# Remainders of the token blocks and of the second weight set on VectorE during the plain products, and a conversion's first two operations never in one step

## The chip, the cores and the metric

One core of one Trainium2 chip. The time is the device time of one execution in microseconds (us); the number quoted is the median of repeated runs. The engines are TensorE (PE in the profile; PEld is its weight load), VectorE (DVE), ScalarE (ACT), GpSimd (POOL) and SyncE (SP), which issues the transfers. Each engine works through its own queue in order; between engines only data dependencies hold work back.

## The reference

Relative-position attention, then a three-way maximum layer. Shapes: batch 4, 8 heads, 576 positions, head size 64; 2304 tokens, model width 512, inner width 768.

```python
scores = scale * q @ k.T + bias          # bias from |i - j| by a small MLP
attn = softmax(scores)                   # rows
x = (attn @ v) as [2304 tokens, 512]
h = max(max(x @ w1, x @ w2), x @ w3)     # 2304 x 768
out = h @ w_out                          # 2304 x 512
```

The three weight matrices and w_out arrive as 64-bit floats.

## The kernel before, in words

**Stages.** Bias setup (to about 57 us); attention, with the conversion of the 64-bit weights beside it (57 to 320 us); products of the tokens with w1, w2, w3 (321 to 525 us); products with w_out (525 us to the end).

**High and low parts.** A product in 32-bit precision is made of three products in a rounded type: a tile is split into a high part (a ScalarE copy that rounds) and a remainder (tile minus high part, a tensor_tensor by the helper `arith`, L415 to L417). Every such remainder, every sum and every elementwise maximum is recorded under L417, so the rows tell them apart by tile names: `b11l` is the remainder of block b11, `wl` that of a weight set, a bare `t` a sum.

**Attention steps.** `Attention.step(n, more)` (L367) is called for n = 0 to 84. Step n emits: the score matmuls of one tile of 128 rows for two heads (`front`, L254; every fifth tile holds the left-over rows of both heads); one to three pieces of attn @ v (`pv`, L347); per head VectorE's `sn` (L264) and ScalarE's exponential `e` (L276); then the side work handed in as `more`, one `next` per entry (L388); then VectorE's reciprocal `rc` (L286) with GpSimd's scaling of `e` (L289) for the step before; the copies of finished pv sums out of PSUM (`split_x`, L363, tile `xb`); and the transposes of step n - 5 (`flip`, L308, L317) with their copies `et` (ScalarE L403, L404; VectorE L406). The pv sum has one PSUM buffer, so the first pv piece of a new sum waits for the `xb` copy of the last. One sum ends in each step with n % 5 == 0, and its copy stands in VectorE's queue behind that step's side work; the next sum begins in the step after.

**Side work.** Generator `first` (`w0`) converts weights. `convert` (L462) is one ScalarE operation (L465: the absolute value, called A here) and four on VectorE (L467 "max", L469 "shift", L472 "or", L475 "fin"), with a yield after each. From step 10 on every step takes one `next` of it, and steps with n % 5 in (0, 4) take two. `early_x` prepares parts of token block 0 from step 45 on, each third step; `late_x` splits b21 and b22 of block 0 (ScalarE high, GpSimd remainder) from step 78 on.

**Token blocks.** The tokens' x is cut into three blocks (x = 0, 1, 2) of four tiles b11, b12, b21, b22 (128 x 768). The class `Blocks` (L423) makes their parts, and four sums t1 to t4 of them, each split as well.

**Weight products.** `moe` (L513) runs 54 items: weight set s times block x. For s = 0 `plain` (L528) multiplies directly, eight `slot()` calls per block. For the others `group` (L539) makes seven products p1, p5, p6, p7, p2, p4, p3 from blocks and sums, one slot after each; each product is 6 matmuls of 384 columns. ScalarE copies p1 and p5 out of PSUM, VectorE adds the others; eight PSUM banks rotate. A slot runs the jobs that stand in the table `jobs` under (item, slot), filled with `at(n, k, ...)` (L584). Slot jobs only set the order of each engine's queue; a later engine can run ahead of TensorE or behind it. Items 0 to 2 are the plain ones; item 3 is set 1 with block 0, and so on. Set 1's parts come from `raise_w` (two ScalarE copies, 768 and 1024 columns) and `lower_w` (remainders). `reload` fetches parked sets from DRAM into the buffers that set 1 leaves.

Of the kernel before, what the change touches and what calls it, by code (L numbers as in the profile page):

```python
# [19 lines left out]
def kernel(  # L20
# [12 lines left out]
    nc = tc.nc  # L33
# [137 lines left out]
    def load_bias(hp, t):  # L171
        if t < NTQ:
            nc.sync.dma_start(out=bias_t[t], in_=bias_rows(128 * t, 128, 2 * hp, 0, S, 2))
        else:
            nc.sync.dma_start(out=bias_t[t][0:LEFT], in_=bias_rows(LB, LEFT, 2 * hp, 0, S))
            nc.sync.dma_start(out=bias_t[t][64:64 + LEFT, 0:LB], in_=bias_rows(LB, LEFT, 2 * hp + 1, LEFT, LB))
            nc.sync.dma_start(out=bias_t[t][64:64 + LEFT, LB:S], in_=bias_rows(LB, LEFT, 2 * hp + 1, 0, LEFT))
# [5 lines left out]
    NS = NTQ + 1  # L183
# [5 lines left out]
    NSTEP = len(sched)  # L189
    LAG = NS  # L190

    class Attention:
# [174 lines left out]
        def step(self, n, more=()):  # L367
            m, f = n - 1, n - LAG
            nh = 0
            if n < NSTEP:  # L370
                un, t = fronts[n]
                hp, b = units[un]
                if t == 0 and un and un + 2 < len(units):
                    self.load_qk(un + 2)
                if t == 3 and un:
                    self.load_v(un)
                nh = self.heads(n)
                self.front(n)
            if n < NS:
                self.warm(n)  # L380
            for _ in range((1, 3, 2, 2, 2)[n % NS]):
                if self.pvq and n >= LAG + TS + 1:
                    self.pvq.pop(0)()
            back = 0 <= f < NSTEP
            for h in range(nh):
                self.shift(n, h)
                self.expo(n, h)
            for w in more:  # L388
                next(w, None)
            if n < NSTEP and b == border[-1] and hp + 1 < HP:  # L390
                load_bias(hp + 1, t)
            if 0 <= m < NSTEP:
                self.norm(m)
            if n < NSTEP and un + 1 < len(units):
                t0 = 1 if un == 1 else 0
                if t == t0:
                    self.splits = self.prep(un + 1)
                if t0 <= t < t0 + 2:
                    next(self.splits)
            self.split_x()  # L400
            if back:
                tps, left = self.flip(f)
                nc.scalar.copy(*tps[0])  # L403
                nc.scalar.copy(*left)  # L404
                if len(tps) > 1:
                    nc.vector.tensor_copy(*tps[1])  # L406
            if back:
                un, t = sched[f]
                g = 0 if t < TS else 1
                w = 128 * TS if g == 0 else S - 128 * TS  # L410
                if t in (TS - 1, NS - 1):
                    self.queue_pv(un, 128 * TS * g, w, *self.et)


    def arith(eng, out, a, b, op=ALU.subtract):  # L415
        f = lambda x: x.bitcast(F32) if x.dtype == F32R else x
        eng.tensor_tensor(out=out, in0=f(a), in1=f(b), op=op)  # L417
# [44 lines left out]
    def convert(pool, w, out, name):  # L462
        a = pool.tile([128, 512], F32, tag="wa", bufs=1, name=f"wa{name}")
        high, low, t = w[:, :, 1], w[:, :, 0], a.bitcast(U32)
        nc.scalar.activation(a, high.bitcast(F32), ACTF.Abs, scale=2.0 ** 16)  # L465
        yield
        nc.vector.tensor_scalar(out=a, in0=a, scalar1=2.0, scalar2=None, op0=ALU.max)  # L467
        yield
        nc.vector.tensor_scalar(out=t, in0=t, scalar1=3, scalar2=0x7FFFFFFF,  # L469
                                op0=ALU.logical_shift_left, op1=ALU.bitwise_and)  # L470
        yield
        nc.vector.scalar_tensor_tensor(out=t, in0=low, scalar=29, in1=t,  # L472
                                       op0=ALU.logical_shift_right, op1=ALU.bitwise_or)
        yield
        nc.vector.scalar_tensor_tensor(out=out, in0=high, scalar=signm, in1=t,  # L475
                                       op0=ALU.bitwise_and, op1=ALU.bitwise_or)
        yield
# [20 lines left out]
    def part(t, n):  # L498
        return t[:, 256 * n:256 * n + 256]
# [13 lines left out]
    def moe(pool, wpool, x0, xa, xb, raw, sr):  # L513
        ht = pool.tile([128, NX, 5, TW], F32, name="ht", bufs=1)
        hd = h_d.rearrange("(f p) (t n) -> p f t n", p=128, t=2)
        xb_ = [x0] + [Blocks(x, xa, xb) for x in range(1, NX)]
        v, g = nc.vector, nc.gpsimd
# [66 lines left out]
        def at(n, k, *what):  # L584
            jobs.setdefault((n, k), []).extend(what)

        b0, b1, b2 = xb_
        F = lambda f, *a: (lambda: f(*a))
        for k, what in enumerate((
                (F(b1.high, "b11", "b21"),),  # L590
                (F(b1.low, "b11"), F(b1.low, "b21", g)),
                (F(b1.high, "b12", "b22"),),
                (F(b1.low, "b12"), F(b1.low, "b22", g)),
                (F(b2.high, "b11", "b21"),),
                (F(b2.low, "b11"), F(b2.low, "b21", g)),
                (F(b2.high, "b12", "b22"),),
                (F(b2.low, "b12"), F(b2.low, "b22", g)),
                (F(b0.high, "t4"), F(b1.sum, "t1")),
                (F(b0.low, "t4"), F(b1.high, "t1")),
                (F(b1.low, "t1"), F(b1.sum, "t3")),  # L600
                (F(b1.high, "t3"), F(b1.sum, "t2")),
                (F(b1.low, "t3"),),
                (F(b1.sum, "t4"), F(b1.high, "t2"), F(b1.low, "t2", g)),
                (F(b2.sum, "t1"),),
                (F(b2.high, "t1"),),
                (F(b1.high, "t4"), F(b2.low, "t1")),
                (F(b1.low, "t4"),),
                (F(b2.sum, "t3"),),
                (F(b2.high, "t3"), F(b2.sum, "t2")),
                (F(b2.low, "t3"),),  # L610
                (F(b2.sum, "t4"), F(b2.high, "t2")),
                (F(b2.low, "t2"),),
                (),
        )):
            at(k // 8, k % 8, *what)
        at(3, 0, F(b2.high, "t4"))
        at(3, 2, F(b2.low, "t4"))

        made_w = {}

        def raise_w(s, k):
# [5 lines left out]
            else:  # L627
                nc.scalar.copy(wf[s][0][:, 768:1792], sr)

        def lower_w(s, k):  # L630
            raw, sr = made_w[s]
            hi, lo = wf[s]
            r = slice(256 * k, 256 * k + 256)
            arith(g, lo[:, r], part(raw, k + 1) if k < 3 else part(sr, k - 3), hi[:, r])

        def reload(s, k):
            if k == 0:
# [3 lines left out]
            nc.sync.dma_start(out=made_w[s][k], in_=w_d[s - PARK[1], k])  # L641

        made_w[1] = (raw, sr)
        at(1, 2, F(raise_w, 1, 0))
        at(1, 7, F(raise_w, 1, 1))
        for k, (n, y) in enumerate(((1, 3), (1, 4), (1, 6), (2, 1), (2, 2), (2, 4), (2, 6))):
            at(n, y, F(lower_w, 1, k))
        at(0, 0, F(reload, 2, 0))
        at(2, 0, F(reload, 3, 0))
        at(2, 7, F(reload, 2, 1))  # L650
# [1 line left out]
        for s in range(2, NSET):  # L652
            n = 3 * s - 3
# [34 lines left out]
        for s in range(4, NSET):  # L688
            n = 3 * s - 8
# [30 lines left out]
        n = 3 * NSET - 3  # L720
# [35 lines left out]
        n = 3 * NSET - 2  # L756
# [22 lines left out]
        for k in range(NK):  # L779
# [10 lines left out]
            for y in range(parts):  # L790
                r = slice(y * DM // parts, (y + 1) * DM // parts)
# [10 lines left out]
    with tc.manual_schedule():  # L802
# [3 lines left out]
        at = Attention(apool)  # L806
        n = 0
# [30 lines left out]
        last = {}  # L838

        def first():  # L840
# [5 lines left out]
            def conv(out, name):  # L846
                if todo:
                    ahead.append(fetch(wpool, *todo.pop(0)))
                yield from convert(wpool, ahead.pop(0), out.bitcast(U32), name)
# [35 lines left out]
        x0 = Blocks(0, xa, xa)  # L885

        def early_x():
            g = nc.gpsimd
            x0.high("b12")
            yield  # L890
            x0.low("b12", g)
            yield
            x0.high("b11")
            yield
            x0.low("b11", g)
            yield
            x0.sum("t1")
            yield
            x0.high("t1")
            yield  # L900
            x0.low("t1", g)
            yield

        def late_x():
            x0.high("b21")
            yield
            x0.low("b21", nc.gpsimd)
            x0.high("b22")
            yield
            x0.low("b22", nc.gpsimd)  # L910
            yield

        ex, lx = early_x(), late_x()
        while n < NSTEP + LAG:
            more = [w0] if n >= 2 * NS else []
            if n >= 2 * NS and n % NS in (0, 4) and n < NSTEP:
                more.append(w0)
            if n >= 9 * NS - 1 and n % 3 == 0:
                more.append(ex)
            if n >= NSTEP - 2:  # L920
                more.append(lx)
            at.step(n, more)
            n += 1
        while at.pvq:
# [6 lines left out]
        x0.sum("t2")  # L931
        x0.low("t3")
        at.split_x()
        x0.sum("t4")
        x0.high("t2")
        x0.low("t2", nc.gpsimd)
        apool.release()
        psums.pop().release()
        psums.append(ctx.enter_context(tc.tile_pool(name="psum_m", bufs=1, space=PSUM, reuse_waits="tile")))
# [57 lines left out]
```

## Time and profile before

| | us |
|---|---|
| median of 3 runs | 606.13 (605.68 to 606.67) |
| profiled execution | 606.03 |
| its span in the trace | 604.2 |

The profiled execution is 1.83 us longer than its span, which is what lies around the span, and 0.10 us under the median. Engine times overlap; only what TensorE waits for, or what it runs at a lower clock, can be read as lost directly.

### The profile page before, as it was taken

What the parts mean: (1) busy time and instruction counts of PE and PEld (TensorE: products, weight loads), DVE (VectorE), ACT (ScalarE), POOL (GpSimd) and SP (SyncE); (2) the same over time, 40 slices, a digit from 0 to 9 for tenths busy, and PEclk for the clock granted to TensorE, in tenths of its full rate; (3) what the DMA queues carried; (4) which work ended last, traced back from release to release, by engine and by line L of the source; (5) the groups of instructions that cost most, each with busy time, mean ns of one, the idle gap of its engine ahead of it and who ended that gap; (6) DMA issues with size and microseconds to landing.
All of it is one profiled execution on the core that took longest, in us unless ns stands there. A gap on an engine that the chain in (4) does not pass through costs nothing.

```text
span 604.2 us, 12112 instructions
## 1 busy us (share of the span) xinstructions
PE 583.6 (97%) x4360; PEld 469.6 (78%) x4360; DVE 438.3 (73%) x891; ACT 347.2 (57%) x800; POOL 330.1 (55%) x325
## 2 busy tenths in 40 slices
PE   8999999989999999999999989999999999999997
PEld 4456766666667666666668989999999999988886
DVE  7995778777788898887638779998999766722211
ACT  7997887878778888888756362223122122232322
POOL 2703765857555777768445546769677865600000
PEclk9999999999999999999999989999999999999999
DMA  5897455724584267510010042242113211754541
GB/s 169 245 333 266 151 159 163 239 85 163 160 249 139 71 192 205 152 38 21 22 36 1 1 140 69 89 140 69 36 57 119 88 36 35 227 184 142 169 149 70
DMA packets 70188, 76.70 MB, mean 127 GB/s; under 512 B 23152, under 2 KB 51184, under 8 KB 70128
## 3 DMA queue, kind: packets, MB, share of 16 engines
q1 hardware_dynamic: 69984, 75.64, 40.4%
q8 instruction: 34, 0.56, 0.4%
q10 hardware_dynamic: 144, 0.29, 0.2%
q14 instruction: 26, 0.21, 0.1%
HBM read 49.56 MB, written 26.36 MB: 126 GB/s over the span
## 4 chain that ended last, share of the span: by engine, by line
PE 67%; DVE 7%; issue 2%; ACT 2%; POOL 1%; DMA 1%; DVEq 0%; ACTq 0%; POOLq 0%
PE p L526 10%; PE pv L347 10%; PE p L524 10%; PE p L525 10%; PE tp L308 8%; PE s L254 7%; PE o L795 4%; PE o L798 4%; PE o L796 4%; DVE t L417 1%; DVE sn L264 1%; PE lp L317 1%; DVE b12l L417 1%; DVE xb L363 1%; DMA w64o<-in_moe_w_out_dram 1%
## 5 line engine op out<-in xcount | busy, mean ns | idle before, releaser
L289 POOL TENSOR_SCALAR e<-e,rc 128x576 f32<-128x576 f32 x144 | 106.1, 749 | 71.9 <-DVE rc L286 41.3
L276 ACT ACTIVATE e<-sn,nm 128x576 f32<-128x576 f32 x144 | 111.0, 773 | 43.5 <-DVE nm L264 41.0
L264 DVE CUSTOM_DVE_ANT_0 sn<-s,bias 128x576 f32<-128x576 f32 x128 | 91.7, 754 | 29.5 <-PE s L254 27.7
L308 PEld LDWEIGHTS tp<-ident,e 128*128 128x128 f32 x576 | 61.4, 141 | 36.0 <-issue 24.0
L308 PE MATMUL tp<-ident,e 128*128 128x128 f32 x576 | 81.2, 281 | 1.8 <-ACT et L403 0.8
L347 PE MATMUL pv<-et,vt 128*64 128x256 f32 (+1 forms) x496 | 73.6, 417 | 8.2 <-DVE xb L363 8.1
L553 ACT COPY m<-p 128x384 f32<-128x384 f32 x24 | 11.5, 481 | 90.2 <-PE p L526 40.9
L406 DVE COPY et<-tp 128x512 f32<-128x512 f32 x64 | 43.8, 685 | 22.5 <-PE tp L308 22.4
L254 PE MATMUL s<-kh,qh 64*128 64x288 f32 (+1 forms) x288 | 57.4, 343 | 1.5 <-ACT bs L158 0.9
L223 POOL TENSOR_TENSOR kl<-kr,kh 128x640 fp32r<-128x640 f32 x16 | 35.5, 2220 | 42.6 <-ACT kh L222 42.5
L347 PEld LDWEIGHTS pv<-et,vt 128*64 128x64 f32 x496 | 31.0, 136 | 30.4 <-issue 9.2
L417 DVE TENSOR_TENSOR hl<-hin,hh 128x768 fp32r<-128x768 f32 x18 | 18.2, 1010 | 50.1 <-ACT hh L751 50.1
L561 POOL TENSOR_TENSOR q<-mp,m 128x768 f32<-128x768 f32 x18 | 33.3, 1848 | 33.3 <-DVE mp L417 32.3
L403 ACT COPY et<-tp 128x512 f32<-128x512 f32 x80 | 45.9, 574 | 6.4 <-PE tp L308 6.4
L254 PE MATMUL s<-kl,qh 64*128 64x288 f32 (+1 forms) x288 | 48.8, 293 | 0.0
L254 PE MATMUL s<-kh,ql 64*128 64x288 f32 (+1 forms) x288 | 48.2, 290 | 0.0
L417 DVE TENSOR_TENSOR ht<-ht,q 128x768 f32<-128x768 f32 x36 | 45.5, 1303 | 0.0
L795 PE MATMUL o<-woh,hh 128*128 128x512 f32 (+1 forms) x114 | 43.4, 385 | 0.0
L138 PE MATMUL bp<-hid,w2s 128*32 128x79 f32 (+51 forms) x640 | 41.1, 391 | 2.1 <-DVE hid L117 1.8
L796 PE MATMUL o<-wol,hh 128*128 128x512 f32 (+1 forms) x114 | 43.0, 381 | 0.0
L254 PEld LDWEIGHTS s<-kh,qh 64*128 64x128 f32 (+1 forms) x288 | 31.5, 184 | 13.5 <-issue 7.1
L799 ACT COPY ot<-o 128x512 f32<-128x512 f32 (+1 forms) x19 | 10.7, 564 | 54.1 <-PE o L798 54.1
(175 smaller groups left out, 1534.9 us busy)
## 6 DMA issues: line engine op xcount, KB each, us to landing
bias_d<-bs SPq DMA_DIRECT2D x36, 295.5 KB, 5.9
bias<-bias_d SPq DMA_DIRECT2D x16, 576.0 KB, 4.1
w<-in_moe_w_dram SPq DMA_DIRECT2D x36, 256.0 KB, 3.9
h_d<-ht SPq DMA_DIRECT2D x18, 384.0 KB, 2.8
hin<-h_d SPq DMA_DIRECT2D x18, 384.0 KB, 3.9
qr<-in_qd_dram SPq DMA_DIRECT2D x16, 320.0 KB, 4.8
kr<-in_kd_dram SPq DMA_DIRECT2D x16, 320.0 KB, 5.0
out_dram<-ot SPq DMA_DIRECT2D x17, 256.0 KB, 4.0
```

The lines of the kernel that those rows point to most:

```text
L254: nc.tensor.matmul(ss[h][:, x, 0:HALF], lhsT=u[q][p, r], rhs=u[k][p, c:c + HALF], start=(j == 0), stop=(j == 2))
L264: nc.vector.tensor_tensor_reduce(out=sn.rearrange("p (a b) -> p a b", a=2), in0=st["s"][h][:, :, 0:HALF], in1=bt.rearrange("p (a b) -> p a ...
L276: nc.scalar.activation(st["e"][:, S * h:S * h + S], sn, ACTF.Exp, scale=-1.0, bias=nm, accum_out=st["sm"][:, h:h + 1])
L289: nc.gpsimd.tensor_scalar(out=e, in0=e, scalar1=rc[:, h:h + 1], scalar2=1.0, op0=ALU.mult, op1=ALU.mult)
L308: nc.tensor.transpose(tp[:, 128 * c:128 * c + 128], e2[:, k0:k0 + 128], ident)
L347: nc.tensor.matmul(pv[p], lhsT=w, rhs=x, start=(c == 0), stop=(c == NTQ))
L417: eng.tensor_tensor(out=out, in0=f(a), in1=f(b), op=op)
L524: nc.tensor.matmul(o, lhsT=hi[:, c], rhs=h[:, j], start=first and j == 0, stop=False)
L525: nc.tensor.matmul(o, lhsT=hi[:, c], rhs=l[:, j], start=False, stop=False)
L526: nc.tensor.matmul(o, lhsT=lo[:, c], rhs=h[:, j], start=False, stop=last and j == 1)
L795: nc.tensor.matmul(po, lhsT=hh[:, f], rhs=woh[:, r], start=(f == 0), stop=False)
L796: nc.tensor.matmul(po, lhsT=hh[:, f], rhs=wol[:, r], start=False, stop=False)
```

## The change

1. In `step`: if a side job that was just advanced yields "scalar", no further side job is advanced in that step. `convert` yields "scalar" after A. So A and the VectorE "max" that reads it never stand in one step, and later calls shift by one each time this bites.
2. `early_x` is put ahead of the conversion calls; `late_x` runs from step 82 on (before: 78), also first.
3. In the plain products every remainder of blocks 1 and 2 is on VectorE (five were on GpSimd: b21l and b22l of blocks 1 and 2, t2l of block 1), t2l of block 0 as well, and all seven remainders of weight set 1 move from GpSimd to two wide VectorE operations (768 and 1024 columns).
4. Order of the jobs: blocks 0's t4 sum and t2 parts move from ahead of `moe` into slots of item 0; set 1's copies to (2, 2) and (2, 3), its remainders to (2, 4) and (2, 5); the last sums of block 2 to items 3 and 4.

```diff
+            last = None
             for w in more:
-                next(w, None)
+                if last != "scalar":
+                    last = next(w, None)
...
         nc.scalar.activation(a, high.bitcast(F32), ACTF.Abs, scale=2.0 ** 16)
-        yield
+        yield "scalar"
...
-        def lower_w(s, k):
-            raw, sr = made_w[s]
+        def lower_w(s, k, eng=g, n=1):
+            src, o = (made_w[s][0], 256) if k < 3 else (made_w[s][1], -768)
             hi, lo = wf[s]
-            r = slice(256 * k, 256 * k + 256)
-            arith(g, lo[:, r], part(raw, k + 1) if k < 3 else part(sr, k - 3), hi[:, r])
+            r = slice(256 * k, 256 * (k + n))
+            arith(eng, lo[:, r], src[:, r.start + o:r.stop + o], hi[:, r])
...
+                (F(b1.high, "b11", "b21"), F(b0.sum, "t4")),
+                (F(b1.low, "b11"), F(b1.high, "b12"), F(b0.high, "t2")),
+                (F(b1.low, "b21"), F(b1.high, "b22")),
+                (F(b1.low, "b12"),),
+                (F(b1.low, "b22"), F(b2.high, "b11")),
+                (F(b0.low, "t2"), F(b2.high, "b21")),
+                (F(b1.sum, "t1"), F(b2.high, "b12")),
+                (F(b2.low, "b11"), F(b2.high, "b22"), F(b1.high, "t1")),
+                (F(b2.low, "b21"), F(b0.high, "t4")),
+                (F(b2.low, "b12"),),
+                (F(b2.low, "b22"),),
+                (F(b0.low, "t4"),),
+                (F(b1.low, "t1"),),
+                (F(b1.sum, "t3"),),
+                (F(b1.sum, "t2"), F(b1.high, "t3")),
+                (F(b1.low, "t3"),),
+                (F(b1.sum, "t4"), F(b1.high, "t2")),
+                (F(b1.low, "t2"), F(b1.high, "t4")),
+                (F(b1.low, "t4"), F(raise_w, 1, 0)),
+                (F(b2.sum, "t1"), F(raise_w, 1, 1)),
+                (F(lower_w, 1, 0, v, 3), F(b2.high, "t1")),
+                (F(lower_w, 1, 3, v, 4),),
+                (F(b2.low, "t1"),),
+                (F(b2.sum, "t3"),),
         )):
             at(k // 8, k % 8, *what)
-        at(3, 0, F(b2.high, "t4"))
-        at(3, 2, F(b2.low, "t4"))
+        at(3, 0, F(b2.sum, "t2"), F(b2.high, "t3"))
+        at(3, 1, F(b2.low, "t3"))
+        at(3, 3, F(b2.sum, "t4"), F(b2.high, "t2"))
+        at(3, 4, F(b2.low, "t2"))
+        at(3, 5, F(b2.high, "t4"))
+        at(4, 2, F(b2.low, "t4"))
...
-        at(1, 2, F(raise_w, 1, 0))
-        at(1, 7, F(raise_w, 1, 1))
-        for k, (n, y) in enumerate(((1, 3), (1, 4), (1, 6), (2, 1), (2, 2), (2, 4), (2, 6))):
-            at(n, y, F(lower_w, 1, k))
...
+            if n >= 9 * NS - 1 and n % 3 == 0:
+                more.insert(0, ex)
             if n >= 2 * NS and n % NS in (0, 4) and n < NSTEP:
                 more.append(w0)
-            if n >= 9 * NS - 1 and n % 3 == 0:
-                more.append(ex)
-            if n >= NSTEP - 2:
-                more.append(lx)
+            if n >= NSTEP + 2:
+                more.insert(0, lx)
...
         at.split_x()
-        x0.sum("t4")
-        x0.high("t2")
-        x0.low("t2", nc.gpsimd)
```

The old table of jobs of the plain products stands in the kernel above (L589 to L617).

## Rows read from the trace of the kernel before

**Rows 1.** The page's busy times: us, share of the span, instructions.

```profile
PE 583.6 (97%) x4360; PEld 469.6 (78%) x4360; DVE 438.3 (73%) x891; ACT 347.2 (57%) x800; POOL 330.1 (55%) x325
```

**Rows 2.** Who waited for whom: total us, times, longest us.

```profile
PE pv L347 <- DVE xb L363: 8.1, 7, 1.7
...
DVE wa L467 <- ACT wa L465: 3.7, 2, 1.9
```

**Rows 3.** TensorE's timeline, first pv pieces: start, us, instruction, [idle before <-releaser].

```profile
96.71 1.57 PE L347 MATMUL pv<-et,vt 128*64 128x320 f32 x10 [1.51 <-DVE xb L363]
...
129.81 1.84 PE L347 MATMUL pv<-et,vt 128*64 128x320 f32 x12 [1.66 <-DVE xb L363]
...
162.75 1.83 PE L347 MATMUL pv<-et,vt 128*64 128x320 f32 x12 [1.51 <-DVE xb L363]
...
179.37 1.83 PE L347 MATMUL pv<-et,vt 128*64 128x320 f32 x12 [0.82 <-DVE xb L363]
...
195.15 1.83 PE L347 MATMUL pv<-et,vt 128*64 128x320 f32 x12
...
211.48 1.84 PE L347 MATMUL pv<-et,vt 128*64 128x320 f32 x12
...
261.75 1.83 PE L347 MATMUL pv<-et,vt 128*64 128x320 f32 x12 [0.84 <-DVE xb L363]
...
277.43 1.83 PE L347 MATMUL pv<-et,vt 128*64 128x320 f32 x12
```

**Rows 4.** VectorE's timeline in four of the attention steps.

```profile
95.84 0.43 DVE L467 TENSOR_SCALAR wa<-wa 128x512 f32<-128x512 f32 x1 [1.86 <-ACT wa L465]
...
193.80 0.74 DVE L475 SCALAR_TENSOR_TENSOR wso<-w64o,signm,wao 128x512 uint32<-128x512 uint32 x1
...
210.15 0.42 DVE L467 TENSOR_SCALAR wao<-wao 128x512 f32<-128x512 f32 x1
210.60 0.43 DVE L469 TENSOR_SCALAR wao<-wao 128x512 uint32<-128x512 uint32 x1
...
222.57 1.88 DVE L467 TENSOR_SCALAR wa<-wa 128x512 f32<-128x512 f32 x1
```

**Rows 5.** TensorE's timeline, end of attention.

```profile
306.91 0.63 PE L308 MATMUL tp<-ident,e 128*128 128x128 f32 x4 [0.57 <-ACT et L404]
```

**Rows 6.** TensorE's timeline, items 3 to 5 (first product of each, and the waits).

```profile
346.46 0.34 PE L524 MATMUL p<-b11h,wh 128*128 128x384 f32 x1
...
349.14 0.44 PE L524 MATMUL p<-t1h,wh 128*128 128x384 f32 x1 [1.46 <-ACT wh L628]
...
357.64 0.44 PE L524 MATMUL p<-b11h,wh 128*128 128x384 f32 x1
...
365.05 0.34 PE L524 MATMUL p<-b11h,wh 128*128 128x384 f32 x1
...
372.35 0.34 PE L524 MATMUL p<-b11h,wh 128*128 128x384 f32 x1
```

**Rows 7.** Busy us (instructions) per engine by stretch, granted clock, DMA share, GB/s.

```profile
321.40:346.50 25.10, 25.10 (x145) 25.10 (x146) 20.13 (x13) 13.80 (x22) 16.70 (x9) 1.00 0.00 1
...
352.00:353.00 1.00, 1.00 (x5) 1.00 (x4) 0.96 (x2) 0.09 (x1) 1.00 (x2) 0.50 0.00 0
```

**Rows 8.** VectorE's timeline in the plain products and after.

```profile
321.25 0.95 DVE L417 TENSOR_TENSOR t<-xb,t 128x768 f32<-128x768 f32 x1
...
330.92 2.60 DVE L417 TENSOR_TENSOR b12l<-xb,b12h 128x768 fp32r<-128x768 f32 x1
...
335.97 0.95 DVE L417 TENSOR_TENSOR t4l<-t,t4h 128x768 fp32r<-128x768 f32 x1
```

**Rows 9.** GpSimd's timeline: beside a conversion, and in the plain products.

```profile
222.35 1.83 POOL L417 TENSOR_TENSOR b11l<-xb,b11h 128x768 fp32r<-128x768 f32 x1
...
330.14 2.56 POOL L417 TENSOR_TENSOR b21l<-xb,b21h 128x768 fp32r<-128x768 f32 x1
...
349.16 4.25 POOL L417 TENSOR_TENSOR wl<-ws,wh 128x256 fp32r<-128x256 f32 x4 [2.70 <-ACT wh L628]
```

More of the change, by code (lines that the diff above doesn't have):

```diff
@@ L585, in at @@
             jobs.setdefault((n, k), []).extend(what)
[L587 to L615, printed above, removed]
-        at(3, 0, F(b2.high, "t4"))
-        at(3, 2, F(b2.low, "t4"))
         made_w = {}
@@ L628, in raise_w @@
                 nc.scalar.copy(wf[s][0][:, 768:1792], sr)
-        def lower_w(s, k):
-            raw, sr = made_w[s]
+        def lower_w(s, k, eng=g, n=1):
+            src, o = (made_w[s][0], 256) if k < 3 else (made_w[s][1], -768)
             hi, lo = wf[s]
-            r = slice(256 * k, 256 * k + 256)
-            arith(g, lo[:, r], part(raw, k + 1) if k < 3 else part(sr, k - 3), hi[:, r])
+            r = slice(256 * k, 256 * (k + n))
+            arith(eng, lo[:, r], src[:, r.start + o:r.stop + o], hi[:, r])
+        b0, b1, b2 = xb_
+        F = lambda f, *a: (lambda: f(*a))
+        for k, what in enumerate((
+                (F(b1.high, "b11", "b21"), F(b0.sum, "t4")),
[22 more added lines that the diff above has]
+                (F(b2.sum, "t3"),),
+        )):
+            at(k // 8, k % 8, *what)
+        at(3, 0, F(b2.sum, "t2"), F(b2.high, "t3"))
[4 more added lines that the diff above has]
+        at(4, 2, F(b2.low, "t4"))
         def reload(s, k):
```

## The prediction

> **What bounds the kernel now.** First the page's busy times: TensorE is busy in 97% of the span [rows 1], so only its waits, or a lower clock, can be won; the other engines have room. Next the list of who waited for whom: in attention TensorE's largest wait is for VectorE's copy `xb`, 8.1 us in seven waits, and VectorE itself waited for A, ScalarE's first operation of a conversion; the row for `wa` has two such waits, and two more like it stand on `wao` [rows 2]. Then TensorE's timeline at the first pv pieces of a sum, to see which waits are long [rows 3]: three of 1.51 to 1.66 us (4.68 together), four of about 0.8 (the remaining 3.4), and none at 195.15, 211.48 and 277.43. Last, TensorE's timeline where the plain products end: item 3 starts at 346.46, stops 1.46 us before p5 and lasts until 357.64 (11.18 us), where item 5 takes 7.30 (365.05 to 372.35) [rows 6]. The windows show why a 1.5 us gap cost more: at 352 us the granted clock was 0.50, which is 1.2 of 2.4 GHz, after TensorE had stood still at 347.7 to 349.1 [rows 6, 7].
>
> So the change can win in two places: 8.1 us of pv waits, and 11.18 - 7.30 = 3.88 us in item 3.
>
> **The skip of a conversion call.** I counted the yields from step 10 on. In the steps with n % 5 == 0, whose VectorE work stands ahead of `xb`, the two calls give before: A and max in steps 15, 25, 35; two VectorE operations in 40 (shift, or), 50 (max, shift), 55, 60, 65 (or, fin); one in 45; none in 20, 30, 70. That is the pattern of the waits [rows 3]: the three long ones follow 15, 25 and 35, the four shorter ones 40, 55, 60, 65; after 45 (one, 195.15), 50 (211.48) and 70 (277.43) there is none. After the change: step 15 A alone; 25 and 35 fin, then A; 40, 55, 60, 65 max and shift; 50 A alone; 45 and 70 or and fin; 20 and 30 as before.
>
> - Steps 15, 25, 35: VectorE sat 1.86 us before max until A came [rows 4]. That goes. What is left is nothing or one fin, 0.74 us in its row, after which no wait followed (at 195.15) [rows 3, 4]: gain 4.68.
> - Steps 40, 55, 60, 65: or and fin become max and shift, 0.42 and 0.43 [rows 4], a pair after which no wait is shown at 211.48 [rows 3]. I leave 0.1 each for what the row can't resolve: 3.4 - 0.4 = gain 3.0.
> - Steps 45 and 70 get the pair or, fin that costs about 0.8 elsewhere [rows 3]: loss 1.6. Bounds: 0 (were there more slack) and 2.0.
> - Smaller: from 96.71 to 277.43 are eleven units, 180.72 us; at the wait-free unit of 15.68 (261.75 to 277.43) they would be 172.5 [rows 3]. The difference of 8.2 is 1.6 more than the six waits between (8.1 - 1.5), so ends of waits and late copies lose something that no row names. I take 0.4 as won, bounds 0 and 1.6.
>
> Moved past: where A goes a step later it lands in a step with no more ScalarE casts than steps 15, 25 and 35 had (A and one high part of k). The conversion has 75 steps and 28 double calls for 88 yields; even with each of its 14 A ending a step it is through by step 74, before the attention ends. The fetches and stores that stand in it go out up to five steps later on SP; nothing in attention reads them.
>
> **late_x four steps later.** TensorE waited 0.57 us at 306.91 for ScalarE's `et`, ahead of which `late_x` had put the high part of b22 [rows 5]. That goes to steps without exponentials. Gain 0.57. The cover: steps 82 to 84 are the last three, some 3.1 us each (15.68 / 5); GpSimd's two remainders there take about 1.83 us each [rows 9] with nothing else queued. Were they late, item 0 would wait for b21 by as much.
>
> **Plain products.** GpSimd's remainders and VectorE's hold each other up: a VectorE operation on 128 x 768 took 2.60 us at 330.92 beside GpSimd's 2.56, and 0.95 where GpSimd was idle (335.97) [rows 8, 9]. After the change GpSimd has no job from its last b22l to the first group's `q`. VectorE has, from the t4 sum (321.25 before [rows 8]) up to the second wide weight remainder, 22 operations; at 0.95, and 0.3 more for the 1024-wide one, 21.2 us; I add 2 us for four places where it waits for a ScalarE high part that stands behind a PSUM copy. So set 1's last remainder is ready at 321.25 + 23.2 = 344.5 on the old axis. TensorE needs it in p5, one product (7.30 / 7 = 1.04) and two matmuls after 346.46: 347.8. Slack 3.3 us, so the wait of 1.46 and the half-clock matmuls behind it go: item 3 falls to 7.30, gain 3.88. Before, the last of these remainders was on GpSimd until 349.16 + 4.25 = 353.4 [rows 9].
>
> Costed at nothing: ScalarE's highs, same number, 13.80 of 25.1 us busy before [rows 7]; block 2's t2, t3, t4 sums and remainders in items 3 and 4 (five or six times 0.95 to 1.5 beside adds of half a us), needed in item 5, whose t2 product is over two items after item 3 starts, 16 us; the eight PSUM banks cover a VectorE that is some us late. If that cover went, the price would be one late product per us. SP: the reloads into set 1's buffers wait for its remainders, which end 8.9 us earlier (353.4 to 344.5), so set 2 comes sooner; nothing new is queued behind them.
>
> **Sum.** 4.68 + 3.0 - 1.6 + 0.4 + 0.57 + 3.88 = 10.9 us. From the profiled execution, 606.03: 595.1; it is 0.10 under the median, so 595.2. After item 3 TensorE runs without a wait until the output stage, so what is won stays won.
>
> **Rivals.**
>
> *Held pairs.* The moved max can be slow: at 222.57 it took 1.88 us beside GpSimd's subtraction of 1.83 us, against 0.42 [rows 4, 9]. The Trainium skill (SBUF — State Buffer, SBUF: two separate sides) says why this could be usual: VectorE and GpSimd share a pair of ports, and the one that starts first keeps it for its whole instruction. By that rule any GpSimd operation under way would hold max back; the trace agrees at 222.57. In steps 40, 55, 60, 65 each pair would then be 1.5 us longer, with waits of 1.4 in place of 0.1 to 0.2: 4 x 1.4 = 5.6 less gain, 600.8. Against it: in these steps GpSimd's next scaling waits for `rc`, which stands behind the pair, and at 210.15 max was short [rows 4]. Chance 0.08.
>
> *Item 3 still waits.* Set 1's wide remainders or their ScalarE sources come after 347.8 by over a us, and the clock falls again: the 3.88 is not won, 599.1. For it: the remainder is now at the end of a chain of 22 on one engine. Chance 0.12.
>
> *The waits in attention only move.* The calls skipped come back as pairs in other steps, 45 and 70 and more, and the waits add up to what they were: only 0.57 + 3.88 is won, 601.6. This is the case in which the skip does not do what it says. Against it: the A and max pairs fell in just four steps and cost 1.86 each [rows 2, 4], no new pair waits on another engine. Chance 0.06.
>
> *Slower: VectorE becomes the bound of the plain products.* Place: set 1's remainders, 22nd in its queue. At d us per operation they are ready at 321.25 + 22 d; past 347.8 TensorE stands still in p5, and the low clock after the stop costs about 2.4 us more (3.88 less the wait of 1.46). All gains together are 10.9, so it decides at a stall of 10.9 - 2.4 = 8.5 us, d = 1.6. With half of them at 2.60 and half at 0.95 [rows 8], d = 1.78: ready at 360.4, stall 12.6, 606.1 - 10.9 + 2.4 + 12.6 = 610.2. For it: 13 operations took 20.13 us before, 1.55 each [rows 7]. Against it: those were beside GpSimd, busy 16.70 of the 25.1 us, and GpSimd is now empty there. Chance 0.04.
>
> **How the numbers follow.** Forecast 0.70, the four rivals 0.08, 0.12, 0.06, 0.04. The forecast's own range: with no new waits in 45 and 70, and 1.2 more of the unnamed loss, 2.8 lower, 592.4, both at once unlikely, so 592.8; upward 0.4 and 0.4 for the bounds, and up to 0.5 each for the four pairs, 598. To hold 8 in 10 it takes in the rival at 599.1: 592.8 to 599.6; left out are about the two at 600.8 and 601.6 and the slower one. A measurement of this kernel can tell about 0.2% from no change. All cases but the last are faster by more: faster 0.95, same 0.01, slower 0.04.
>
> **What would show it.** Right: no VectorE wait for A; of the seven pv waits only two of some 0.8 us, after steps 45 and 70; item 0 starts about 7 us earlier; VectorE's 128 x 768 operations there at 0.95 and GpSimd empty; item 3 at 7.3 us with a granted clock of 1.00. Wrong: max at 1.9 in the moved pairs; a TensorE wait for `wl` or `wh` in p5; VectorE late enough in items 3 to 5 that TensorE waits for a PSUM bank, of which no row shows one now; or a lower clock in a stretch where TensorE did not wait.

## The result, and the profile after

The kernel after takes 596.5 us (median of 4 runs, 595.74 to 597.28) against 606.4 for the kernel before (4 runs): a ratio of 0.9837, interval 0.9819 to 0.9855. The forecast was 595.2 with a range of 592.8 to 599.6. The profiled execution took 595.74, its span is 594.0, 10.2 less than before.

The page's engine times, beside [rows 1]: GpSimd lost 20 us of work (13 remainders), VectorE gained under 2 us, though it took all of them over, as eight operations.

```profile
PE 580.3 (98%) x4360; PEld 468.1 (79%) x4360; DVE 440.1 (74%) x899; ACT 348.0 (59%) x800; POOL 310.0 (52%) x312
```

Who waited for whom, beside [rows 2]: no row of VectorE waiting for A is left, and the pv waits for `xb` fell from 8.1 to 3.1 us. Another 1.0 us in three waits of pv is put down to TensorE's own `s`.

```profile
PE pv L347 <- DVE xb L363: 3.1, 5, 0.8
```

TensorE's timeline in attention, beside [rows 3] (the first pv pieces of a sum in steps 16, 36, 41, 46, 51, 56, 58, 61, 66, 71, 76):

```profile
94.36 1.83 PE L347 MATMUL pv<-et,vt 128*64 128x320 f32 x12
...
157.26 1.84 PE L347 MATMUL pv<-et,vt 128*64 128x320 f32 x12
173.28 1.83 PE L347 MATMUL pv<-et,vt 128*64 128x320 f32 x12 [0.17 <-PE s L254]
189.81 1.83 PE L347 MATMUL pv<-et,vt 128*64 128x320 f32 x12 [0.77 <-DVE xb L363]
205.48 1.84 PE L347 MATMUL pv<-et,vt 128*64 128x320 f32 x12
222.13 1.83 PE L347 MATMUL pv<-et,vt 128*64 128x320 f32 x12 [0.52 <-DVE xb L363]
230.03 1.08 PE L347 MATMUL pv<-et,vt 128*64 128x256 f32 x8 [0.59 <-PE s L254]
239.15 1.84 PE L347 MATMUL pv<-et,vt 128*64 128x320 f32 x12 [0.60 <-DVE xb L363]
255.50 1.84 PE L347 MATMUL pv<-et,vt 128*64 128x320 f32 x12 [0.60 <-DVE xb L363]
271.86 1.84 PE L347 MATMUL pv<-et,vt 128*64 128x320 f32 x12 [0.61 <-DVE xb L363]
287.55 1.83 PE L347 MATMUL pv<-et,vt 128*64 128x320 f32 x12
```

The long waits are gone. After steps 55, 60 and 65 there is still 0.5 to 0.6, which the forecast put at 0.1. After 45 and 70 there is 0.77 and 0.61, where it had 0.8 each. And 0.59 stands before the pv of step 58, which it had not named.

TensorE's timeline at item 0 and items 3 to 5, beside [rows 6]. Item 0 starts 6.33 us earlier than the 321.39 of before (forecast: about 7); item 3 takes 347.43 - 340.12 = 7.31 us, with no wait.

```profile
315.06 0.44 PE L526 MATMUL c<-b11h,wh 128*128 128x384 f32 x1 [1.16 <-DVE xb L363]
...
340.12 0.34 PE L526 MATMUL p<-b11h,wh 128*128 128x384 f32 x1
...
347.43 0.33 PE L526 MATMUL p<-b11h,wh 128*128 128x384 f32 x1
...
354.73 0.34 PE L526 MATMUL p<-b11h,wh 128*128 128x384 f32 x1
```

The window of the plain products, beside [rows 7] (busy us and instructions of PE, PEld, DVE, ACT, POOL; granted clock; DMA share; GB/s): 24 VectorE operations in 20.97 us, where 13 took 20.13; GpSimd empty.

```profile
315.10:340.10 25.00, 25.00 (x144) 25.00 (x145) 20.97 (x24) 16.32 (x26) 0.00 (x0) 1.00 0.03 5
```

VectorE's timeline there, beside [rows 8]: 0.95 us for 128 x 768, and set 1's last remainder ready at 337.94 + 1.22 = 339.16. On the axis of before (6.33 later) that is 345.5; the forecast was 344.5. p5 wants it at 340.12 + 1.4 = 341.5.

```profile
315.79 0.95 DVE L419 TENSOR_TENSOR b11l<-xb,b11h 128x768 fp32r<-128x768 f32 x1
...
337.94 1.22 DVE L419 TENSOR_TENSOR wl<-ws,wh 128x1024 fp32r<-128x1024 f32 x1
```

**Where the 10.2 us are.** By starts in the two traces: up to the pv of step 11, 0.78 (79.46 to 78.68; as much, 71.02 to 70.23, at the pv of step 8, ahead of the first changed call, so it is how this stage differs between executions); steps 11 to 76, 213.65 to 208.87, 4.78; from there to item 0, 28.28 to 27.51, 0.77; items 0 to 2 nothing; item 3, 11.18 to 7.31, 3.87; the rest, 246.56 and 246.57, nothing.

### The profile page after: what moved, and what is told of

Read it like the earlier page. It is cut to its first block, busy times and chain, and to the rows that moved or that the text cites. A ratio compares the mean times of both kernels' runs of the same rounds, so it can differ in the third digit from the quotient of the medians.

```text
span 594.0 us, 12090 instructions
## 1 busy us (share of the span) xinstructions
PE 580.3 (98%) x4360; PEld 468.1 (79%) x4360; DVE 440.1 (74%) x899; ACT 348.0 (59%) x800; POOL 310.0 (52%) x312
## 4 chain that ended last, share of the span: by engine, by line
PE 91%; ACT 4%; DVE 3%; issue 2%; DVEq 0%
PE pv L347 14%; PE s L254 12%; PE tp L308 12%; PE p L526 10%; PE p L528 10%; PE p L527 10%; PE o L797 4%; PE o L800 4%; PE o L798 4%; PE bp L138 3%; PE c L526 1%; PE c L528 1%; PE c L527 1%; ACT hid L120 1%; ACT bs L158 1%
## 5 line engine op out<-in xcount | busy, mean ns | idle before, releaser
L419 POOL TENSOR_TENSOR wl<-wr,wh 128x256 fp32r<-128x256 f32 x25 | 23.6, 955 | 41.4 <-ACT wh L596 38.0
```

## The experiments

The time of a single execution moves with the first stage: the pv of step 8 starts between 70.23 and 72.40 us in the fourteen traces, ahead of every call that an edit touches. So verdicts rest on stretches inside a trace. Runs 1, 2, 3 and 5 have four executions each, the others one. "Steps 16 to item 0" is from the first pv after step 15 to item 0: 220.70 us in the kernel after.

**1. Attention alone.** The kernel before with the skip and `early_x` first.

```diff
+                if last != "scalar":
+                    last = next(w, None)
...
+        yield "scalar"
...
+                more.insert(0, ex)
```

> The kernel before with the skip of a conversion call and early_x ahead, and nothing else. Theory (two separate gains): attention is shorter by the 5.6 to 5.9 us that the profile after shows up to the last step, item 3 still lasts 11.2 us with its stop before p5 and a granted clock of 0.5 behind it; time 600.5, ratio 0.990 to 0.991. Rival (the shift of the queues alone cures item 3): item 3 at 7.3 us, 597. Rival (the skip only moves the waits): 605.5 or more.

601.89 us, ratio 0.9917 (0.990 to 0.9933): for attention the theory, with a gain of 4.9 us where it had 5.6 to 5.9, which took in the 0.78 of the first stage. Attention's pv waits are those of after. But item 3 was a surprise. TensorE's timeline and the windows:

```profile
342.39 0.34 PE L526 MATMUL p<-b11h,wh 128*128 128x384 f32 x1
...
345.05 0.44 PE L526 MATMUL p<-t1h,wh 128*128 128x384 f32 x1 [1.45 <-ACT wh L630]
...
353.56 0.44 PE L526 MATMUL p<-b11h,wh 128*128 128x384 f32 x1 [1.49 <-ACT ht L538]
```

```profile
347.00:348.00 1.00, 1.00 (x8) 0.93 (x7) 1.00 (x2) 0.00 (x0) 1.00 (x2) 1.00 0.00 0
```

The same stop of 1.45 us, and the clock stayed at 1.00; yet item 3 lasted 11.17 us, as before. TensorE waited 1.49 us for a PSUM bank, the one whose copy `ht` stood in ScalarE's queue behind t2h of block 2. The kernel before has the same copy in the same place, right ahead of item 4 at 357.64:

```profile
357.12 0.47 ACT L536 COPY ht<-c 128x384 f32<-128x384 f32 x1
```

It ended at 357.59. So the low clock of before had cost nothing of its own: it filled time in which the bank would have been waited for.

**2. Plain products alone.** The kernel after with the attention steps of before.

```diff
-                if last != "scalar":
-                    last = next(w, None)
+                next(w, None)
...
```

(`early_x` and `late_x` go back to their places and steps of before as well)

> The kernel after with the attention steps of before (calls, early_x and late_x). Theory: the seven pv waits of 8.1 us are all there, GpSimd is empty in items 0 to 2, VectorE's 128 x 768 operations take 0.95 us, item 3 lasts 7.3 us at a clock of 1.00; gain 3.9, time 602.5, ratio 0.9935. Rival (the gains are not separate): item 3 still waits, 605 or more.

602.67 us, ratio 0.9931 (0.9913 to 0.9949). The pv waits were 8.1 us in seven again, item 3 went from 347.40 to 354.71, 7.31 us. The two gains are separate and add up: 0.83% and 0.69% against 1.63% together. What is missing, 0.11%, is about the 0.77 us (0.13%) from step 76 to item 0, where `late_x` stands: neither run 1 nor run 2 moves it.

**3. Second conversion call in steps 1 and 3 of five.**

```diff
-            if n >= 2 * NS and n % NS in (0, 4) and n < NSTEP:
+            if n >= 2 * NS and n % NS in (1, 3) and n < NSTEP:
```

> The kernel after with the second conversion call in the steps with n % 5 in (1, 3) in place of (0, 4), so that no step whose VectorE queue holds an xb copy (n % 5 of 0 or 2) has two VectorE operations of side work. Theory: what is left of pv waits after the change (3.1 us in five waits, 0.6 before the pv of step 58, and the matching parts of the units over 15.7 us, 4.8 us in all) comes from such pairs; they go, time 592 to 593. Rival (the pairs just delay other copies, et or e, in the steps they move to): 595 to 597, with new waits at tp. Rival slower: pairs in steps 1 and 3 hold up sn and TensorE's score matmuls wait for PSUM: over 597.

596.51 us, ratio 0.9834 (0.9817 to 0.9851): nothing gained, and "Steps 16 to item 0" took 221.16 us. It is the first rival in part: its time, but without its waits at `tp`. The waits behind the steps with n % 5 == 0 are gone but for 0.15, and others stand before the second pv sum of every five steps, which waits for the `xb` copy in a step with n % 5 == 2 (where the row names TensorE's own `s`, the copy was still the last to end):

```profile
134.59 1.08 PE L347 MATMUL pv<-et,vt 128*64 128x256 f32 x8 [0.70 <-DVE xb L363]
...
166.81 1.08 PE L347 MATMUL pv<-et,vt 128*64 128x256 f32 x8 [0.79 <-PE s L254]
...
232.32 1.08 PE L347 MATMUL pv<-et,vt 128*64 128x256 f32 x8 [1.02 <-PE s L254]
```

VectorE's timeline before the first of them shows how: max took 1.77 us (at 128.05) in the step with n % 5 == 1, and "or" 1.87 us (at 132.21) in the next, each beside a GpSimd subtraction of 1.55 and 1.57 us; beside none, max takes 0.42 [rows 4]. VectorE had no idle time from the one to the copy at 134.07, so what the pair ran late was carried on, and the slow "or" added to it. How much each of the two cost the run does not separate.

**4. late_x from step 78 again.**

```diff
-            if n >= NSTEP + 2:
-                more.insert(0, lx)
+            if n >= NSTEP - 2:
+                more.append(lx)
```

> The kernel after with late_x from step 78 on again, last in the list. Theory: TensorE's wait of about 0.6 us at tp for ScalarE's et comes back near the end of attention and the unit that ends there is 0.7 us longer; time 0.5 to 0.7 us over the kernel after. Rival (late_x cost nothing by itself): same chain as after, no wait of tp for et, same time.

The wait is back, 0.56 us of `tp` for `et`, and the stretch from the pv of step 76 to that of step 81 took 14.46 us against 13.70: 0.76. The theory. (The execution took 596.71 us.)

```profile
301.51 0.63 PE L308 MATMUL tp<-ident,e 128*128 128x128 f32 x4 [0.56 <-ACT et L406]
```

**5. Second call in steps 3 and 4, early_x from step 50.**

```diff
-            if n >= 9 * NS - 1 and n % 3 == 0:
+            if n >= 10 * NS and n % 3 == 0:
...
-            if n >= 2 * NS and n % NS in (0, 4) and n < NSTEP:
+            if n >= 2 * NS and n % NS in (3, 4) and n < NSTEP:
```

> The kernel after with the second conversion call in the steps with n % 5 in (3, 4), and early_x from step 50 on, so that no pair of VectorE operations stands in a step with n % 5 of 0, 1 or 2. Theory (what is left of the pv waits comes from VectorE being late at the xb copies of steps 0 and 2, and a pair in step 1 is carried into step 2, which the run with 1 and 3 showed as waits before the second sum): a pair in 3 is worked off in step 4, which has one sn in place of two; the waits go, item 0 starts 3 us or more earlier than after (315.06), time 593. Rival (VectorE has no step with room, wherever the pairs stand, and a single operation beside GpSimd's 1.55 us subtraction is as long as a pair): waits of 2 us or more in all, 595.5 or more.

594.69 us, ratio 0.9815 (0.9798 to 0.9831), 0.3% under the kernel after by medians and 0.2% by the ratios, and the two intervals overlap, so the times alone leave it open. The trace is clearer: from step 16 to item 0 it took 218.40 us, 2.30 less than after. The theory's direction, less than its 3 us. What is left is short and of several kinds:

```profile
237.34 1.84 PE L347 MATMUL pv<-et,vt 128*64 128x320 f32 x12 [0.18 <-PE s L254]
244.93 1.08 PE L347 MATMUL pv<-et,vt 128*64 128x256 f32 x8 [0.27 <-DVE xb L363]
249.16 0.63 PE L308 MATMUL tp<-ident,e 128*128 128x128 f32 x4 [0.22 <-DVE et L408]
```

**6. The split of block 2's t2 behind the last plain copy.** In the kernel before:

```diff
-                (F(b2.sum, "t4"), F(b2.high, "t2")),
-                (F(b2.low, "t2"),),
+                (F(b2.sum, "t4"),),
+                (),
...
-        at(3, 0, F(b2.high, "t4"))
+        at(3, 0, F(b2.high, "t2"), F(b2.high, "t4"))
+        at(3, 1, F(b2.low, "t2"))
```

> The kernel before with the split of block 2's t2 three slots later, behind ScalarE's copy of the last plain product, and nothing else. It leaves the stop before p5 as it is. Theory (half of what item 3 lost was a PSUM bank: item 4's first product waits for the copy of the last plain product, which stood behind t2h and through it behind VectorE's sums; with attention alone the clock stayed at 1.00 and item 3 was as long): item 3 lasts 9.0 us if the clock holds and up to 10.7 if it falls, with no wait before item 4; time 0.5 to 2.2 us under before. Rival (item 3 lost its time to the stop and the clock behind it, as the prediction said): 11.2 us as before.

605.54 us, 0.6 under before. Item 3 lasted 355.24 - 345.73 = 9.51 us at a clock of 1.00, with the stop of 1.45 still there and no wait before item 4. Run 1, at the same clock, has 11.17. So the bank wait is real and goes by the place of one ScalarE operation. Of the 1.66 us, 0.67 come back in item 4 (8.07 us; in run 1 it has 7.40), which now waits for a later bank. The 9.51 is 0.5 over the theory: beside 7.30, the stop and a wait of 0.20 for `wl`, 0.56 is left, which no row names, though the clock was full.

```profile
357.99 0.44 PE L524 MATMUL p<-t2h,wh 128*128 128x384 f32 x1 [0.51 <-DVE mp L417]
```

**7. A stop made by repeating a remainder.** The kernel after with set 1's first remainder made six times.

```diff
-                (F(lower_w, 1, 0, v, 3), F(b2.high, "t1")),
+                (*[F(lower_w, 1, 0, v, 3)] * 6, F(b2.high, "t1")),
```

> The kernel after with set 1's first remainder on VectorE made six times in place of once (five repeats of 0.87 us ahead of the second one). Theory: slack was 2.4 us (339.1 to 341.5), so TensorE stops 2.0 us in p5 for the remainder, item 3 lasts 9.3 us with no bank wait; whether the clock falls after such a stop is open, it would add up to 1.7 us. Time 2.0 to 3.7 over the kernel after. Rival (the banks or ScalarE bind before the remainder does): item 3 over 11 us at a clock of 1.00.

The stop came already in p1, which reads the repeated part, and was 2.42 us; item 3 lasted 353.93 - 342.36 = 11.57 us with no bank wait. Here the clock fell and did cost: 11.57 - 7.31 - 2.42 = 1.84 us. An estimate of what of it is the clock's: run 6 lost 0.56 past its two named waits at full clock, 0.28 each, so 1.84 less one such loss, about 1.6. TensorE's timeline, then the window behind the stop:

```profile
345.29 0.45 PE L528 MATMUL p<-b11h,wl 128*128 128x384 f32 x1 [2.42 <-DVE wl L419]
```

```profile
347.00:348.00 1.00, 1.00 (x5) 1.00 (x4) 1.00 (x2) 0.00 (x0) 0.00 (x0) 0.50 0.79 307
```

The execution took 602.22 us; of that 2.2 us lie ahead of item 0 (at 317.27), so the stretch counts.

**8. Set 1's remainders on GpSimd.**

```diff
-                (F(lower_w, 1, 0, v, 3), F(b2.high, "t1")),
-                (F(lower_w, 1, 3, v, 4),),
+                (*(F(lower_w, 1, k) for k in range(3)), F(b2.high, "t1")),
+                tuple(F(lower_w, 1, k) for k in range(3, 7)),
```

> The kernel after with set 1's seven remainders on GpSimd again, in the same slots (2, 4) and (2, 5). Theory (what matters is that block remainders left GpSimd and the chain got ahead, not that VectorE does set 1's): GpSimd starts them at 336 and has the one of p5 by 340, before 341.5; VectorE's last plain operations take 1.5 us beside them in place of 0.95; item 3 stays at 7.3 us, same time as after. Rival (set 1 must be on VectorE): a stop in p5 of 1 us or more, item 3 over 8.3 us.

596.03 us, item 3 from 340.44 to 347.74: 7.30, no wait. By itself this part of the change is not needed for item 3.

**9. Four block remainders on GpSimd.**

```diff
-                (F(b1.low, "b21"), F(b1.high, "b22")),
+                (F(b1.low, "b21", g), F(b1.high, "b22")),
```

(and b22 of block 1, b21 and b22 of block 2 in the same way)

> The kernel after with the remainders of b21 and b22 of blocks 1 and 2 on GpSimd again, as before, in the slots of after. Theory (VectorE and GpSimd hold each other up in operations with two tiles from SBUF, so the four are not saved but cost VectorE about as much in stretching): VectorE's first remainders take about 2.6 us again beside GpSimd's 2.6, the last remainder of set 1 ends between 340.5 and 343.5 on the axis of after in place of 339.1; item 3 between 7.3 and 9.3 us. Rival (two engines share the work and the chain gets shorter): last remainder of set 1 by 337, VectorE's operations under 1.3 us.

596.2 us. VectorE's operation beside GpSimd's is at 2.60 us again:

```profile
316.25 2.60 DVE L419 TENSOR_TENSOR b11l<-xb,b11h 128x768 fp32r<-128x768 f32 x1
```

Set 1's last remainder was ready 340.12 - 315.52 = 24.60 us after item 0 began, against 24.10 in the kernel after; that is 339.66 on the axis of after, under the 340.5 to 343.5 of the theory. Four operations taken off VectorE, and its chain ends 0.5 us later: they are not saved, they are paid in stretching. Item 3 is at 7.30, the slack covers it.

**10. Set 0's remainders on VectorE.**

```diff
-                    arith(nc.gpsimd, part(lo, k), part(raw, k), part(hi, k))
+                    arith(nc.vector, part(lo, k), part(raw, k), part(hi, k))
```

> The kernel after with the four remainders of set 0 (made in steps 58 to 64, 256 columns each) on VectorE in place of GpSimd. Theory (the shift took 0.86 us in steps 60 and 65, and the pairs there cost 0.6 of pv wait, because GpSimd's scaling of e was late behind those remainders and ran beside the shift): the shift takes 0.43 in steps 60 and 65 and the pv waits after them fall from 0.60 to 0.2 or less. Rival (the pair costs 0.6 by itself): 0.6 stays.

The cause is as the theory has it: the shift is back at 0.43 us, and the pv after steps 60 and 65 (240.28, 257.37) have no wait. (A wait of `tp`, 0.32 us, stands just ahead of the first; it could hide that much of a pv wait, not the 0.60.) Time is not won: "Steps 16 to item 0" took 222.16 us, 1.46 more than after. `tp` waits for ScalarE's `et`, 0.25 and 0.32 us around step 60 and 0.30 before step 65, and VectorE itself stood 1.83 us before the first moved remainder, for ScalarE's `wh`. The execution took 597.92 us.

```profile
238.39 0.42 DVE L469 TENSOR_SCALAR wa<-wa 128x512 f32<-128x512 f32 x1
238.84 0.43 DVE L471 TENSOR_SCALAR wa<-wa 128x512 uint32<-128x512 uint32 x1
```

```profile
234.84 0.63 PE L308 MATMUL tp<-ident,e 128*128 128x128 f32 x4 [0.25 <-ACT et L405]
238.60 0.66 PE L308 MATMUL tp<-ident,e 128*128 128x128 f32 x4 [0.32 <-ACT et L405]
```

After 8 and 9 I formed another theory: that the order of the jobs, not the engine, had cured item 3. Two runs put it to the test.

**11. Order alone.** The kernel after, every moved remainder back on GpSimd: the edits of 8 and 9 and

```diff
-                (F(b0.low, "t2"), F(b2.high, "b21")),
+                (F(b0.low, "t2", g), F(b2.high, "b21")),
...
-                (F(b1.low, "t2"), F(b1.high, "t4")),
+                (F(b1.low, "t2", g), F(b1.high, "t4")),
```

> The kernel after with all the remainders that it moved put back on GpSimd (b21 and b22 of blocks 1 and 2, t2 of blocks 0 and 1, set 1), in the order of jobs of after. Theory (the order of the jobs made the gain in item 3: set 1's ScalarE copies and the copy of the last plain product no longer stand behind a t1h or t2h that waits for a chain of both engines; set 1 alone and four block remainders alone on GpSimd cost nothing): item 3 lasts 7.3 to 8.3 us. Rival (each move alone has slack but together VectorE's place is needed): a stop before p5 or a bank wait, item 3 over 9 us.

The theory fell. Item 3 lasted 352.10 - 340.85 = 11.25 us, with a stop of 1.73 us before p5's remainder and a granted clock of 0.50 behind it. TensorE's timeline, then VectorE's: VectorE sat 4.23 us for GpSimd's t2l early in the stage, and never got ahead. The execution took 600.38 us.

```profile
344.16 0.44 PE L528 MATMUL p<-t1h,wl 128*128 128x384 f32 x1 [1.73 <-POOL wl L419]
```

```profile
324.61 2.60 DVE L419 TENSOR_TENSOR t<-xb,xb 128x768 f32<-128x768 f32 x1 [4.23 <-POOL t2l L419]
```

**12. Engines alone.** The kernel before, the same remainders on VectorE, its order of jobs and its attention kept.

```diff
-                (F(b1.low, "b11"), F(b1.low, "b21", g)),
+                (F(b1.low, "b11"), F(b1.low, "b21")),
...
-            arith(g, lo[:, r], part(raw, k + 1) if k < 3 else part(sr, k - 3), hi[:, r])
+            arith(v if s == 1 else g, lo[:, r], part(raw, k + 1) if k < 3 else part(sr, k - 3), hi[:, r])
```

(b22 and t2 of block 1, b21 and b22 of block 2, t2 of block 0 likewise)

> The kernel before with the same remainders on VectorE, set 1's seven in pieces of 256, in the order of jobs of before, and the attention of before. Theory (order): ScalarE's t1h and t2h of block 2 still wait for VectorE's sums with set 1's second copy and the last plain copy behind them, but the 2.95 us in which VectorE waited for GpSimd's t2l are gone; item 3 between 8 and 11 us. Rival (the engine alone is the gain): item 3 at 7.3 us.

The rival: item 3 takes 7.30 us in the old order (the execution took 601.92 us). ScalarE's copy `wh`, for which the kernel before stopped in p5, ran at 342.07:

```profile
346.33 0.34 PE L524 MATMUL p<-b11h,wh 128*128 128x384 f32 x1
...
353.63 0.33 PE L524 MATMUL p<-b11h,wh 128*128 128x384 f32 x1
```

```profile
342.07 1.05 ACT L628 CAST wh<-ws 128x1024 fp32r<-128x1024 f32 x1
```

The engine is the gain in item 3, the new order is not needed for it. 8 and 9 had only shown that either half of the move has slack by itself.

## Why the prediction was right, and where it was not

| step of the sum | forecast | measured in the profiled executions |
|---|---|---|
| steps 15, 25, 35 | 4.68 | 4.71 |
| steps 40, 55, 60, 65 | 3.0 | 0.60 + 0.30 - 0.29 + 0.24 = 0.85 |
| steps 45, 70 | -1.6 | -0.75 - 0.68 = -1.43 |
| unnamed | 0.4 | 0.66 - 0.01 = 0.65 |
| late_x (step 76 to item 0) | 0.57 | 0.77 |
| item 3 | 3.88 | 3.87 |
| first stage, untouched | 0 | 0.78 |
| sum | 10.9 | 10.2 |

Each attention entry is the length of units, before less after; a unit is the five steps from one first pv of 320 columns to the next. The first entry is all of steps 11 to 36.

That the sum came so close is in part luck. The four pairs won 2.15 us less than forecast; 0.78 of what made up for it lies in the first stage, which the change does not touch, and 0.62 in three other attention terms that came out better (0.17, 0.25, 0.20).

**The skip.** Right. Run 1 holds this part alone; the three 1.5 us waits went because VectorE no longer sat for A, and nothing took their place.

**The pairs max and shift** were the term that was mis-sized. "I leave 0.1 each" rested on one row after which no wait is shown, step 50. The pair in 40 cost 0.17, those in 55, 60 and 65 cost 0.52 to 0.60. In step 60 the shift took 0.86 us in place of 0.43 (in 65 as well, at 254.05):

```profile
237.23 0.42 DVE L469 TENSOR_SCALAR wa<-wa 128x512 f32<-128x512 f32 x1
237.69 0.86 DVE L471 TENSOR_SCALAR wa<-wa 128x512 uint32<-128x512 uint32 x1
```

GpSimd's scaling of `e` was still under way then, late behind a remainder of set 0 that the skip had shifted by two steps:

```profile
235.88 0.73 POOL L419 TENSOR_TENSOR wl<-wr,wh 128x256 fp32r<-128x256 f32 x1
236.59 1.68 POOL L289 TENSOR_SCALAR e<-e,rc 128x576 f32<-128x576 f32 x2
```

The shift ended at 238.55, 0.28 us after the scaling (236.59 + 1.68 = 238.27). The Trainium skill (SBUF — State Buffer, SBUF: two separate sides) has the engine that comes second at the shared port pair wait for the other's whole instruction; the trace agrees: at 222.57 in the kernel before, max too ended 0.27 us after GpSimd's operation [rows 4, 9]. In step 55 it was max, 0.92 us beside a scaling that was late behind a remainder of `early_x` (b11l, 2.27 us at 217.22):

```profile
220.30 0.92 DVE L469 TENSOR_SCALAR wa<-wa 128x512 f32<-128x512 f32 x1
```

Run 10 took set 0's remainders off GpSimd, and the shift was 0.43 us; the wait after step 55, which they have no part in, stayed at 0.52. This is the rival of held pairs, with the mechanism that it named and a third of its price; the argument against it, that GpSimd's scaling waits behind the pair, holds for this step's scaling and not for the one of the step before. Run 10 won no time all the same, since waits for ScalarE came up in its place; no run tried another place for these remainders.

**Step 57.** I counted pairs of conversion operations only in the steps with n % 5 == 0. The t1 sum of `early_x` and fin now meet in step 57, whose queue holds the other sum's copy: 0.59 us before the pv of step 58 (the row names TensorE's own `s`, but the copy ended last, at 229.40 + 0.53 = 229.93). Together with the pairs that is why the unit of step 60 got longer (-0.29). The yields would have shown it.

**The unnamed loss.** Most of it was in one unit, 16.33 to 15.67 us (step 46 to 51): in step 45 A and the b12 high part had stood ahead of ScalarE's `et`. The skip moved A out.

**Item 3.** Right in size and in its main cause: GpSimd's and VectorE's remainders beside each other made the chain late, and on VectorE alone it is ready 2.4 us before p5 (forecast 3.3). Runs 11 and 12 separate the engine from the order. The link to the stop is one that the prediction did not spell out: TensorE stopped for `wh`, ScalarE's copy of set 1 [rows 6], and only 0.20 us more for a remainder. That copy stood behind t1h of block 2, which waited for VectorE's sum, which waited for GpSimd's t2l. From the kernel before:

```profile
345.79 1.48 DVE L417 TENSOR_TENSOR t<-xb,xb 128x768 f32<-128x768 f32 x1 [2.95 <-POOL t2l L417]
...
347.31 0.83 ACT L440 CAST t1h<-t 128x768 fp32r<-128x768 f32 x1 [3.16 <-DVE t L417]
348.05 1.04 ACT L628 CAST wh<-ws 128x1024 fp32r<-128x1024 f32 x1
```

In run 12 the same copy ran 6 us earlier.

Wrong was how I split the 3.88: the wait of 1.46 "and the half-clock matmuls behind it". Run 1 has the stop without the low clock and loses the same 3.87 us, because item 4 then waits for a PSUM bank; run 6 takes the bank wait away. The slower rival's 2.4 us for the clock was built on that split; where no other wait follows, run 7 puts the clock at 1.6 to 1.84 us. The prediction also held that no row shows a wait for a PSUM bank; in the kernel before the bank came free 0.05 us before item 4, just late enough to be hidden.

**What stays open.** Why the clock fell after a stop of 1.46 us in the kernel before, of 1.73 in run 11 and of 2.42 in run 7, and not after 1.45 in runs 1 and 6, was not tried apart. Nor did it fall after the waits of 1.51 to 1.66 us in the attention of the kernel before: the granted clock there is 1.00 throughout.

## What to carry to other kernels

Side work ahead of a copy that frees the only buffer of the bounding engine costs what it has past the slack of that step (by estimate 0.7 to 0.8 us here: one fin of 0.74 cost nothing, a pair of 0.85 in step 40 cost 0.17, one of 1.44 in step 70 cost 0.61): count what falls into each step, over all generators, before moving a call. Two engines that stretch each other are not two engines: eleven more operations on VectorE took 0.8 us more of it once GpSimd was empty. A low clock beside a stop is not its price until the stretch is seen without it; another wait may be hidden in the slow part.

## What the runs showed that I had not expected

The same stop, 1.46 and 1.45 us, was followed by a granted clock of 0.50 in the kernel before and of 1.00 in run 1, and the item was equally long, 11.18 and 11.17 us. And the shortest stretch from step 16 to item 0 belongs to neither of the two kernels but to run 5, with the second conversion call in steps 3 and 4: 218.40 us, and 594.69 us in all.
